# Second attention with three query chunks side by side, and a bit-mask exponential for more key-block pairs on VectorE

## The chip, the cores and the metric

One core of a Trainium2 chip runs the whole program. The metric is the device time of one execution in microseconds, the median of several runs. One further execution was recorded by the hardware profiler; its span, groups, waits and timelines are what this document calls the profile and the trace.

## The reference

Four layers with residuals act on x (2048 tokens, 1024 features, bf16): a linear attention A, a softmax attention B, and both again with the same weights.

```python
x = A_x
x = x + _A_ref(_layernorm(x, axis=-1), A_wqkv, A_w_phi, A_wo)
x = x + _B_ref(_layernorm(x, axis=-1), B_wqkv, B_wo)
x = x + _A_ref(_layernorm(x, axis=-1), A_wqkv, A_w_phi, A_wo)
x = x + _B_ref(_layernorm(x, axis=-1), B_wqkv, B_wo)
```

B is ordinary attention with 32 heads of 32 features: `scores = q k^T * 32**-0.5`, a softmax over 2048 keys, `o = p v`, and a product with wo. A maps q and k by a learned 32x32 matrix per head and two softmaxes over its features, and then needs only sums over keys. B's exponentials, 32 x 2048 x 2048 of them per attention, are the largest body of elementwise work.

## The kernel before, in words

All tokens stay in SBUF as xT, features on partitions, in four chunks of 512 tokens (NC = 4). Heads go in eight groups g of four. A **turn** (qc, g) is one query chunk with one head group, 32 turns in an attention. A turn has two halves pp; a half has 8 key blocks d times 4 strips j. One **unit** (qc, g, pp, d, j) is a score tile of 128 keys by 512 queries from one 32-row strip, 64 units in a turn. Strips 0 and 1 belong to one block of keys, 2 and 3 to another.

`attention` cuts the units into groups of three (WIDE). Each group is three score matmuls on TensorE (L1034), which use different 32-row strips of the array and so run side by side, into one of two sets of three PSUM banks; then one ScalarE exponential over 128x1536 (L1042) into a bf16 tile of class E. Per half, sixteen weighted-sum steps (L1072) add v and ones times these tiles into PSUM bank 6, four matmuls a step, each in its own 32 columns; L1087 copies the bank out. The denominators go through DRAM (L1117 to L1125) and L1128 scales the result into tiles of class oT, which the output projection reads: b_o in the first attention, b_last in the second.

Some units are taken from ScalarE and computed on VectorE by `exp_dve`. EXTRA lists for each attention which (pp, d) of a turn go there, in pairs of units. Each pair has two score matmuls in strip 3 (L972), into bank 7. Then VectorE takes the power of two apart: it rounds the scaled score by adding a large constant (L977), subtracts to get the fraction (L980), clamps the integer part and turns it into exponent bits (L983, L986), evaluates a cubic (three steps at L991) and multiplies (L994).

Projections share bank 7 and TensorE's time with the attention: b_k makes the keys of a group (copied out at L867, spread by four DMAs at L859), b_v the values, b_q the queries of a turn (L875, then two swapping DMAs, L880 and L881). With turns two chunks wide (`turns`, for both attentions: chunks 0 and 1 alternate over the groups, then chunk 2 over all groups, then chunk 3) the queries of chunks 2 and 3 are made early by q_away (L891), stored to DRAM (L893), and fetched by q_back. In the first attention the linear layer that follows is begun beside it (a_keys and layernorm with `alone`), and its weight slabs of 1 MB share SP's queue (L538).

The order of everything is planned when the program is built. `Sched` holds the operations with a planned duration, dependencies, buffers and a due number (`prio`, ten per turn); it plays them through, the lowest due number first among those ready on an engine, within the quotas of buffers by class (QUOTA), and puts fillers on TensorE (L1290) where it would be too little occupied (SPELL, KEEP). The result is one fixed instruction list per engine. Each engine then runs its list in order and waits only by semaphores.

The two lines that set what goes to VectorE and in what order turns run:

```python
EXTRA = (lambda i: [(0, 2), (1, 2)] if 12 <= i < 17 else [],
         lambda i: ([(0, 2), (1, 2)] if i % 3 else [(0, 2), (0, 5), (1, 4)]) if 16 <= i < 30 else [(i % 2, 2)] if 8 <= i < 16 else [])
...
turns = [(qc, g) for g in range(G) for qc in range(2)] + [(qc, g) for qc in range(2, NC) for g in range(G)]
```

Of the kernel before, what the change touches and what calls it, by code (L numbers as in the profile page):

```python
# [10 lines left out]
ACT = mybir.ActivationFunctionType  # L11
# [8 lines left out]
DH = 32  # L20
# [27 lines left out]
class Sched:  # L48
# [96 lines left out]
    def run(self):  # L145
# [25 lines left out]
        while left:  # L171
# [85 lines left out]
NUMS = 2  # L257
LNN = 4
GATE = (1, 1)
KVG = 0.12  # L260
QUOTA = {"pk": 3, "pv": 2, "kv": 1, "ln": 2, "mm": 2, "cmp": 2, "bc": 4, "num": NUMS, "wt": 4, "fil": 2,
         "e": 6, "vp": 6, "e1": 4, "vp1": 4, "E": 6, "q2": 3, "kt": 3, "w2": 8, "w2o": 3, "oT": 26, "T": 4, "den": 2,
         "lnt": 6, "lnw": 2, "lnw1": 1, "eq": 8, "ns": 4, "cw": 6, "hl": 6, "oc": 2, "slab": 7, "slabk": 3, "fin": 4,
         "rs": 8, "pkf": 1, "cden": 2, "part": 8, "w2r": 1,
         "xs": 1, "xu": 2, "xg": 2, "xx": 2, "E1": 3}
SPELL = 3.4
KEEP = 0.75

ROUND = 1.5 * 2**21
POW2_D = 0.32318750170670074  # L270
POW2_0 = 0.998010015430466
POW2_C = (-2.753493604392706, 3.611980637904819, -2.738565741928622)
LEAD = 5.0
EXTRA = (lambda i: [(0, 2), (1, 2)] if 12 <= i < 17 else [],
         lambda i: ([(0, 2), (1, 2)] if i % 3 else [(0, 2), (0, 5), (1, 4)]) if 16 <= i < 30 else [(i % 2, 2)] if 8 <= i < 16 else [])

# [5 lines left out]
def dve_us(n):  # L282
    return n / 960 + 0.15
# [6 lines left out]
def kernel(  # L290
# [19 lines left out]

    q_scale = float(DH**-0.5 / (4 * math.log(2)))

# [646 lines left out]
    def exp_dve(qc, g, pp, d, prio, kT, q_of):  # L959


        u_b, u_v = sb("xu", 2, C512, dt=F32)
        g_b, g_v = sb("xg", 2, C512, dt=F32)
        x_b, x_v = sb("xx", 2, C512, dt=F32)
        e_b, e_v = sb("E1", 2, C512)
        r = slice(96, 128)
        gs = []
        for k in range(2):
            s_b, s_v = ps("xs", FIL)

            def sfn(k=k, s_v=s_v):
                nc.tensor.matmul(  # L972
                    out=s_v(), lhsT=kT[g][1]()[r, pp, (d + k) * P:(d + k + 1) * P],
                    rhs=q_of[(qc, g)][1]()[r, (pp + 1) % 2, :], start=True, stop=True, tile_position=(96, 0))
            so = op("PE", MM, sfn, flat([kT[g][2][(d + k) // 2], q_of[(qc, g)][2]]),
                    [s_b, kT[g][0], q_of[(qc, g)][0]], prio, mode="r")
            uo = op("DVE", dve_us(512), lambda k=k, s_v=s_v: nc.vector.tensor_scalar(  # L977
                out=u_v()[:, k, :], in0=s_v(), scalar1=POW2_D, scalar2=ROUND, op0=ALU.add, op1=ALU.add),
                [so], [s_b, u_b], prio + 0.01)
            gs.append(op("DVE", dve_us(512), lambda k=k, s_v=s_v: nc.vector.scalar_tensor_tensor(  # L980
                out=g_v()[:, k, :], in0=u_v()[:, k, :], scalar=ROUND, in1=s_v(), op0=ALU.subtract, op1=ALU.subtract),
                [uo], [s_b, u_b, g_b], prio + 0.01))
        wo = op("DVE", 1024 / 1920 + 0.15, lambda: nc.vector.tensor_scalar(  # L983
            out=u_v(), in0=u_v(), scalar1=ROUND - 31.5, scalar2=ROUND + 32.0, op0=ALU.max, op1=ALU.min),
            gs, [u_b], prio + 0.02)
        wo = op("DVE", 1024 / 1920 + 0.15, lambda: nc.vector.tensor_scalar(  # L986
            out=u_v().bitcast(I32), in0=u_v(), scalar1=ROUND - 31.75, scalar2=float(2**25),
            op0=ALU.subtract, op1=ALU.mult), [wo], [u_b], prio + 0.02)
        last = gs
        for i, c in enumerate(POW2_C):  # L990
            last = [op("DVE", dve_us(1024), lambda i=i, c=c: nc.vector.scalar_tensor_tensor(  # L991
                out=x_v(), in0=(x_v() if i else g_v()), scalar=c, in1=g_v(), op0=ALU.add, op1=ALU.mult),
                last, [g_b, x_b], prio + 0.02)]
        eo = op("DVE", dve_us(1024), lambda: nc.vector.scalar_tensor_tensor(  # L994
            out=e_v(), in0=x_v(), scalar=POW2_0, in1=u_v(), op0=ALU.add, op1=ALU.mult),
            [wo, *last], [x_b, u_b, e_b], prio + 0.02)
        return eo, (e_b, lambda: e_v().rearrange("p a b -> p (a b)"))

    def attention(base, kT, vT, q_of, gate, extra):
# [7 lines left out]
        for qc, g in turns:  # L1007
            for pp, d in extra(pos[(qc, g)]):
                eo, (e_b, e_v) = exp_dve(qc, g, pp, d, base + 10 * pos[(qc, g)] + 5 * pp + 0.5 * d - LEAD, kT, q_of)
                for k in range(2):  # L1010
                    ex_of[(qc, g, pp, d + k, 3)] = eo
                    e_of[(qc, g, pp, d + k, 3)] = (e_b, e_v, k)
        units = [u for u in units if u not in ex_of]
        n = 0
        i = 0
        while i < len(units):
# [14 lines left out]
            def sfn(grp=grp, s_v=s_v):  # L1031
# [10 lines left out]
            ex = op("ACT", act_us(w * C512), lambda s_v=s_v, e_v=e_v, w=w: nc.scalar.activation(  # L1042
                out=e_v()[:, 0:w * C512], in_=s_v(), func=ACT.Exp, scale=4 * math.log(2)),
                [so], [s_b, e_b], prio - 3)
# [6 lines left out]
        if True:  # L1051
            for qc, g in turns:
                T = []
                end = (qc, g) == turns[-1]
                for pp in range(2):
                    a_b, a_v = ps("acc", [(6,)])
                    last = None
                    for d in range(8):
                        prio = base + 10 * pos[(qc, g)] + 5 * pp + 0.5 * d
                        for u in range(2):  # L1060
# [4 lines left out]
                            def fn(us=us, kc=kc, u=u, d=d, a_v=a_v, v_v=v_v, g=g, pp=pp):  # L1065
                                for k in range(2):
                                    eb, ev, x = e_of[us[k]]
                                    j = 2 * pp + k
                                    for what in range(2):
                                        col = 64 * ((pp + what) % 2) + 32 * k  # L1070
                                        o = (g % 4) * P + j * DH
                                        nc.tensor.matmul(  # L1072
                                            out=a_v()[col:col + 32, :],
                                            lhsT=v_v()[:, kc % 4, o:o + DH] if what == 0 else ones_bf[:],
                                            rhs=ev()[:, x * C512:(x + 1) * C512],
                                            start=(d == 0 and u == 0), stop=(d == 7 and u == 1),
                                            tile_position=(0, col), skip_group_check=True)
# [5 lines left out]
                            last.accum = (d, u) != (7, 1)  # L1083
                    if end and pp:
# [51 lines left out]

    turns = [(qc, g) for g in range(G) for qc in range(2)] + [(qc, g) for qc in range(2, NC) for g in range(G)]
    pos = {t: i for i, t in enumerate(turns)}
    xnA, xnB = {}, {}
# [20 lines left out]
    for layer in range(2):  # L1160
        base = BASE[layer]
        second = base + (100, 45)[layer]
        last = layer == 1
# [36 lines left out]
        for c in range(NC):  # L1200
# [5 lines left out]
            a_out(c, pr + 22, wo_s, oc)  # L1206
            xnB[c] = layernorm(c, pr + 23, ANY, n=LNN if c == NC - 1 else 2)
# [5 lines left out]
        gate = [lnq[-1]] if GATE[layer] else []  # L1213
        at = second + 130

        for g in range(1, G):
            pr = at + 10 * pos[(0, g)] - 19
            w = slab("w2", pr - 1, B_w[:, :, D + g * P:D + (g + 1) * P], P)
            for c in range(NC):
                b_k(g, c, pr + 4 * c, w, kT, FIL, "DVE")  # L1220
        for c in range(NC):
            for t in range(TB):
                b_v(1, c, t, at + 4.5 * (4 * c + t) + 2, bv_s[1], vT, FIL, "DVE")
        for g in range(G):
            pr = at + 10 * pos[(0, g)]
            w = slab("w2", pr - 11, B_w[:, :, g * P:(g + 1) * P], P) if g else wq0
            for qc in range(NC):
                if qc < 2:
                    if qc or g:
                        q_of[(qc, g)] = b_q(g, qc, pr + 10 * qc - 8, w, FIL)  # L1230
                else:
                    away = q_away(g, qc, pr + 2 + 6 * (qc - 2), w, FIL)
                    q_of[(qc, g)] = q_back(g, qc, at + 10 * pos[(qc, g)] - 12, away)
        oTs, last_s = attention(at, kT, vT, q_of, gate, EXTRA[layer])
        if last:
            bo_s = [slab("slab", at + 160 + fc, B_o[:, :, fc * C512:(fc + 1) * C512], C512) for fc in range(2)]
        for qc, p0, gap in ((0, 163, 1.5), (1, 176, 1.5), (2, 251, 1.5)):
            if last:
                gap = (6, 6, 9)[qc]
                p0 = (163, 200, 251)[qc]  # L1240
                for t in range(TB):
# [84 lines left out]
```

## Time and profile before

| what | value |
|---|---|
| median of 3 runs | 2449.53 us (2446.66 to 2449.86) |
| the profiled execution's own time | 2446.52 us |
| its span | 2444.7 us |
| first score exponential of the first, second attention | 354.3 us, 1541.6 us from the span's start |
| ScalarE after the last score exponential of the first attention | next at 1310.7 us |
| score exponentials of three units (L1042) | 1332 |
| fillers on TensorE (L1290) | 2296 matmuls |
| pairs on VectorE | 50 (100 score matmuls at L972) |

How to read the profile: the page gives busy time of each engine over the span and in 40 slices (a digit is tenths of a slice); then groups of instructions by line: count, busy time, mean duration of one in ns, the engine's idle time just before them and what ended it. PE is TensorE's matmuls, PEld its weight loads, DVE VectorE, ACT ScalarE, SP the queue that issues DMAs. A row of the stretches gives its ends and length in us, then busy time with the number of instructions of PE, PEld, DVE, ACT and POOL, the granted clock, and the DMAs' share and GB/s. A row of waits gives who waited for whom, the total in us, how often, and the longest. A timeline row gives start, length, engine, line and operation, and in brackets the idle time before it with what ended it. Matmuls overlap, so their durations (380 ns) are longer than their pitch.

### The profile page before, as it was taken

What the parts mean: (1) busy time and instruction counts of PE and PEld (TensorE: products, weight loads), DVE (VectorE), ACT (ScalarE), POOL (GpSimd) and SP (SyncE); (2) the same over time, 40 slices, a digit from 0 to 9 for tenths busy, and PEclk for the clock granted to TensorE, in tenths of its full rate; (3) what the DMA queues carried; (4) which work ended last, traced back from release to release, by engine and by line L of the source; (5) the groups of instructions that cost most, each with busy time, mean ns of one, the idle gap of its engine ahead of it and who ended that gap; (6) DMA issues with size and microseconds to landing.
All of it is one profiled execution on the core that took longest, in us unless ns stands there. A gap on an engine that the chain in (4) does not pass through costs nothing.

```text
span 2444.7 us, 65791 instructions
## 1 busy us (share of the span) xinstructions
PE 2298.8 (94%) x29160; PEld 848.7 (35%) x29160; DVE 1337.6 (55%) x1775; ACT 2128.3 (87%) x1891; POOL 22.0 (1%) x70
## 2 busy tenths in 40 slices
PE   7999999999989999899999999999999998998998
PEld 4443333333333333333333333333333333333333
DVE  6986752222256635533425766322255478788863
ACT  6336569999999999999996555799999999999998
POOL 0000000000000000000000000000000000000000
PEclk9999999999999999999999999999999999999999
DMA  9210101112111122222324001111121100100000
GB/s 208 62 36 3 31 20 39 39 42 51 37 58 45 45 65 76 75 71 72 123 59 125 1 5 40 32 43 37 40 64 28 37 30 26 35 31 28 27 23 32
DMA packets 204773, 118.59 MB, mean 49 GB/s; under 512 B 122824, under 2 KB 194504, under 8 KB 203720
## 3 DMA queue, kind: packets, MB, share of 16 engines
q1 hardware_dynamic: 203432, 112.29, 17.0%
q8 instruction: 228, 3.74, 0.6%
q10 hardware_dynamic: 1056, 2.10, 0.3%
q14 instruction: 57, 0.47, 0.1%
HBM read 78.71 MB, written 16.24 MB: 39 GB/s over the span
## 4 chain that ended last, share of the span: by engine, by line
ACT 43%; PE 35%; issue 10%; DVE 7%; DMA 3%; SPq 2%; ACTq 0%; DVEq 0%
ACT arena L1042 42%; PE psum L434 19%; PE psum L1072 5%; PE psum L438 4%; PE psum L1034 4%; DVE arena L991 2%; DMA arena<-rd 1%; SPq L469 1%; PE psum L1290 1%; DVE arena L1128 1%; ACT arena L638 1%; PE psum L804 1%; PE psum L671 1%; DVE arena L977 1%; DVE arena L1087 1%
## 5 line engine op out<-in xcount | busy, mean ns | idle before, releaser
L1042 ACT ACTIVATE arena<-psum 128x1536 bf16<-128x1536 f32 x1332 | 1798.7, 1677 | 15.1 <-PE psum L1034 7.6
L1072 PE MATMUL psum<-arena 128*32 128x512 bf16 x4096 | 657.1, 385 | 8.8 <-DVE arena L1087 4.9
L1072 PE MATMUL psum<-arena,ones_bf 128*32 128x512 bf16 x4096 | 656.8, 386 | 2.3 <-issue 2.3
L1034 PE MATMUL psum<-arena 32*128 32x512 bf16 x3996 | 525.1, 383 | 97.1 <-ACT arena L1042 88.9
L438 PE MATMUL psum<-arena 128*32 128x512 bf16 x8256 | 578.6, 381 | 3.8 <-DVE arena L530 0.8
L434 PE MATMUL psum<-arena 128*128 128x512 bf16 x2032 | 472.5, 384 | 10.5 <-DVE arena L1108 3.1
L1034 PEld LDWEIGHTS <-arena 32*128 32x128 bf16 x3996 | 175.5, 91 | 624.6 <-issue 613.1
L434 PEld LDWEIGHTS <-arena 128*128 128x128 bf16 x2032 | 191.0, 98 | 268.7 <-issue 58.2
L438 PEld LDWEIGHTS <-arena 128*32 128x32 bf16 x8256 | 204.1, 96 | 211.4 <-issue 64.8
L1072 PEld LDWEIGHTS <-arena 128*32 128x32 bf16 x4096 | 156.4, 94 | 277.7 <-issue 250.8
L867 DVE CAST arena<-psum 128x512 bf16<-128x512 f32 x112 | 77.2, 689 | 259.2 <-PE psum L438 246.2
L991 DVE SCALAR_TENSOR_TENSOR arena<-arena 128x1024 f32<-128x1024 f32 x150 | 183.4, 1222 | 7.4 <-PE psum L438 2.5
L1290 PE MATMUL psum<-xT,zero 128*32 128x512 bf16 x2296 | 182.9, 380 | 0.0
L1072 PEld LDWEIGHTS <-ones_bf 128*32 128x32 bf16 x4096 | 153.9, 94 | 16.1 <-issue 7.4
L1087 DVE COPY arena<-psum 128x512 f32<-128x512 f32 x126 | 86.6, 687 | 97.3 <-PE psum L1072 96.2
L1128 DVE TENSOR_TENSOR arena<-arena 64x512 bf16<-64x512 f32 x124 | 84.6, 682 | 59.5 <-DMA arena<-rd 46.7
L638 ACT ACTIVATE arena<-psum 128x512 bf16<-128x512 f32 x80 | 42.8, 598 | 79.4 <-PE psum L434 65.7
L651 DVE TENSOR_TENSOR arena<-psum,arena 128x1024 bf16<-128x1024 f32 x64 | 78.3, 1224 | 59.2 <-PE psum L438 53.2
L977 DVE TENSOR_SCALAR arena<-psum 128x512 f32<-128x512 f32 x100 | 68.9, 689 | 69.9 <-PE psum L972 61.8
L642 DVE TENSOR_REDUCE arena<-arena 128x32 f32<-128x1024 bf16 x64 | 77.7, 1214 | 48.6 <-ACT arena L638 48.6
L761 ACT ACTIVATE arena<-psum 128x512 bf16<-128x512 f32 x128 | 69.4, 595 | 34.1 <-PE psum L434 33.6
L526 DVE TENSOR_TENSOR arena<-xT,arena 128x1024 f32<-128x1024 bf16 x64 | 77.9, 1218 | 31.3 <-ACT arena L515 31.2
(102 smaller groups left out, 1295.9 us busy)
## 6 DMA issues: line engine op xcount, KB each, us to landing
arena<-rd SPq DMA_DIRECT2D x62, 256.0 KB
arena<-in_A_wqkv_dram SPq DMA_DIRECT2D x10, 1024.0 KB
arena<-in_B_wqkv_dram SPq DMA_DIRECT2D x32, 256.0 KB
arena<-arena SPq DMA_DIRECT2D x256, 32.0 KB
arena<-in_B_wo_dram SPq DMA_DIRECT2D x32, 256.0 KB
arena<-wd_k SPq DMA_DIRECT2D x8, 1024.0 KB
arena<-in_B_wqkv_dram SPq DMA_DIRECT2D x4, 1024.0 KB
arena<-arena SPq DMA_DIRECT2D x64, 64.0 KB
```

Source lines behind the costliest of these rows:

```text
L434: nc.tensor.matmul(out_, lhsT=lhsT, rhs=rhs, start=start, stop=stop, skip_group_check=True)
L438: nc.tensor.matmul(out_[ks, :], lhsT=lhsT[:, ks], rhs=rhs, start=start, stop=stop, tile_position=(0, 32 * k), skip_group_check=True)
L526: s1 = op("DVE", dve_us(1024), lambda pr=pr, w_v=w_v: nc.vector.tensor_tensor(out=w_v(), in0=xT[:, pr, csl(c)], in1=m_v().unsqueeze(1).to_ ...
L651: ml = op("DVE", dve_us(1024), lambda vpv=vpv, wv_=wv_, sv=sv: nc.vector.tensor_tensor(out=wv_()[:, :, :, 0:DH], in0=vpv().rearrange("p (h ...
L977: uo = op("DVE", dve_us(512), lambda k=k, s_v=s_v: nc.vector.tensor_scalar(out=u_v()[:, k, :], in0=s_v(), scalar1=POW2_D, scalar2=ROUND, o ...
L991: last = [op("DVE", dve_us(1024), lambda i=i, c=c: nc.vector.scalar_tensor_tensor(out=x_v(), in0=(x_v() if i else g_v()), scalar=c, in1=g_ ...
L1034: nc.tensor.matmul(out=s_v()[:, x * C512:(x + 1) * C512], lhsT=kT[g][1]()[r, pp, d * P:(d + 1) * P], rhs=q_of[(qc, g)][1]()[r, (pp + j // ...
L1042: ex = op("ACT", act_us(w * C512), lambda s_v=s_v, e_v=e_v, w=w: nc.scalar.activation(out=e_v()[:, 0:w * C512], in_=s_v(), func=ACT.Exp, s ...
L1072: nc.tensor.matmul(out=a_v()[col:col + 32, :], lhsT=v_v()[:, kc % 4, o:o + DH] if what == 0 else ones_bf[:], rhs=ev()[:, x * C512:(x + 1) ...
L1087: cp = op("DVE", dve_us(512), lambda t_v=t_v, a_v=a_v: nc.vector.tensor_copy(out=t_v(), in_=a_v()), [last], [a_b, t_b], prio - 4)
L1128: s = [op("DVE", dve_us(512), lambda a=a, k=k, o_v=o_v, r_v=r_v, T=T: nc.vector.tensor_tensor(out=o_v()[a, :], in0=T[k][1]()[a, :], in1=r_ ...
L1290: nc.tensor.matmul(psum[32 * k:32 * k + 32, 6 * C512:7 * C512], lhsT=zero[:], rhs=xT[:, 0, 0:C512], start=False, stop=False, tile_position ...
```

## The change

- In the second attention three chunks run side by side (SIDE): turns go over chunks 0, 1 and 2 for each head group, then chunk 3 over all groups. No queries go through DRAM there; those of chunk 3 are made by b_q one turn ahead (LATE), with their weight slabs loaded again. The values of the second half of the heads (VGAP), the output projections (OP0, OGAP) and their slabs (BO) get new due numbers. The first attention keeps two chunks.
- VectorE takes strips 2 and 3 of one key block (d) where it took strip 3 of two blocks (d, d+1). The weighted-sum steps of those pairs go last in their half, so that start and stop follow the order n.
- The exponential itself: the score, scaled by 2**23/ln 2 in q_scale, is added to a constant and clamped at 0 with an int32 output (one step per unit from PSUM); one mask takes the mantissa and sets the exponent of 1, another keeps the exponent; three cubic steps and a product follow.
- EXTRA: 18 pairs in the first attention (turns 10 to 18, two each) and 54 in the second (turns 3 to 29, two each).
- Keys are due five earlier; quotas and one planned duration (KVG) are set anew.

```diff
-KVG = 0.12
+KVG = 0.14
...
-         "xs": 1, "xu": 2, "xg": 2, "xx": 2, "E1": 3}
+         "xs": 1, "xu": 2, "xg": 1, "xx": 1, "E1": 3}
...
+SIDE = (2, 3)
+VGAP = 7.0
+LATE = 10.0
+BO = 225
+OP0 = (233, 259, 285)
+OGAP = (3.2, 3.2, 3.2)
+EXTRA = (lambda i: [(0, 2), (1, 2)] if 10 <= i < 19 else [],
+         lambda i: [(0,2),(1,4)] if 3 <= i < 30 else [])
...
-    q_scale = float(DH**-0.5 / (4 * math.log(2)))
+    q_scale = float(DH**-0.5 / math.log(2) * BITS)
...
-                    out=s_v(), lhsT=kT[g][1]()[r, pp, (d + k) * P:(d + k + 1) * P],
-                    rhs=q_of[(qc, g)][1]()[r, (pp + 1) % 2, :], start=True, stop=True, tile_position=(96, 0))
+                    out=s_v(), lhsT=kT[g][1]()[r, pp, d * P:(d + 1) * P],
+                    rhs=q_of[(qc, g)][1]()[r, (pp + 1) % 2, :], start=True, stop=True,
+                    tile_position=(64 + 32 * k, 0))
...
-            uo = op("DVE", dve_us(512), lambda k=k, s_v=s_v: nc.vector.tensor_scalar(
-                out=u_v()[:, k, :], in0=s_v(), scalar1=POW2_D, scalar2=ROUND, op0=ALU.add, op1=ALU.add),
-                [so], [s_b, u_b], prio + 0.01)
-            gs.append(op("DVE", dve_us(512), lambda k=k, s_v=s_v: nc.vector.scalar_tensor_tensor(
-                out=g_v()[:, k, :], in0=u_v()[:, k, :], scalar=ROUND, in1=s_v(), op0=ALU.subtract, op1=ALU.subtract),
-                [uo], [s_b, u_b, g_b], prio + 0.01))
+            ys.append(op("DVE", dve_us(512), lambda k=k, s_v=s_v: nc.vector.tensor_scalar(
+                out=y_v()[:, k, :].bitcast(I32), in0=s_v(), scalar1=POW2_B, scalar2=0.0, op0=ALU.add, op1=ALU.max),
+                [so], [s_b, y_b], prio + 0.01))
+        mo = op("DVE", 1024 / 1920 + 0.15, lambda: nc.vector.tensor_scalar(
+            out=m_v().bitcast(I32), in0=y_v().bitcast(I32), scalar1=0x7FFFFF, scalar2=0x3F800000,
+            op0=ALU.bitwise_and, op1=ALU.bitwise_or), ys, [y_b, m_b], prio + 0.02)
+        po = op("DVE", 1024 / 1920 + 0.15, lambda: nc.vector.tensor_scalar(
+            out=y_v().bitcast(I32), in0=y_v().bitcast(I32), scalar1=0x7F800000, scalar2=None,
+            op0=ALU.bitwise_and), [mo], [y_b], prio + 0.02)
...
+                    own = extra(pos[(qc, g)])
+                    order = [(d, u) for d in range(8) for u in range(2) if not (u and (pp, d) in own)]
+                    order += [(d, 1) for d in range(8) if (pp, d) in own]
...
+        wide = SIDE[layer]
+        turns = [(qc, g) for g in range(G) for qc in range(wide)] + [(qc, g) for qc in range(wide, NC) for g in range(G)]
...
-            pr = at + 10 * pos[(0, g)] - 19
+            pr = at + 10 * pos[(0, g)] - 24
...
-                b_k(g, c, pr + 4 * c, w, kT, FIL, "DVE")
+                b_k(g, c, pr + 2 * wide * c, w, kT, FIL, "DVE")
...
-                else:
+                elif wide == 2:
...
+        if wide == 3:
+            for g in range(G):
+                pl = at + 10 * pos[(NC - 1, g)] - LATE
+                after = q_of[(NC - 1, g - 2) if g > 1 else (2, G - 1)][2][0]
+                wl = slab("w2", pl - 3, B_w[:, :, g * P:(g + 1) * P], P, [after])
+                q_of[(NC - 1, g)] = b_q(g, NC - 1, pl, wl, FIL)
```

More of the change, by code (lines that the diff above doesn't have):

```diff
@@ L983, in exp_dve @@
[L983 to L989, printed above, removed]
+            ys.append(op("DVE", dve_us(512), lambda k=k, s_v=s_v: nc.vector.tensor_scalar(
+                out=y_v()[:, k, :].bitcast(I32), in0=s_v(), scalar1=POW2_B, scalar2=0.0, op0=ALU.add, op1=ALU.max),
+                [so], [s_b, y_b], prio + 0.01))
@@ new lines, in exp_dve @@
+        mo = op("DVE", 1024 / 1920 + 0.15, lambda: nc.vector.tensor_scalar(
[4 more added lines that the diff above has]
+            op0=ALU.bitwise_and), [mo], [y_b], prio + 0.02)
+        last = [mo]
@@ L990, in exp_dve @@
         for i, c in enumerate(POW2_C):
             last = [op("DVE", dve_us(1024), lambda i=i, c=c: nc.vector.scalar_tensor_tensor(
-                out=x_v(), in0=(x_v() if i else g_v()), scalar=c, in1=g_v(), op0=ALU.add, op1=ALU.mult),
-                last, [g_b, x_b], prio + 0.02)]
+                out=x_v(), in0=(x_v() if i else m_v()), scalar=c, in1=m_v(), op0=ALU.add, op1=ALU.mult),
+                last, [m_b, x_b], prio + 0.02)]
         eo = op("DVE", dve_us(1024), lambda: nc.vector.scalar_tensor_tensor(
-            out=e_v(), in0=x_v(), scalar=POW2_0, in1=u_v(), op0=ALU.add, op1=ALU.mult),
@@ L996, in exp_dve @@
-            [wo, *last], [x_b, u_b, e_b], prio + 0.02)
+            out=e_v(), in0=x_v(), scalar=POW2_0, in1=y_v(), op0=ALU.add, op1=ALU.mult),
+            [po, *last], [x_b, y_b, e_b], prio + 0.02)
         return eo, (e_b, lambda: e_v().rearrange("p a b -> p (a b)"))
@@ L1042, in attention @@
             ex = op("ACT", act_us(w * C512), lambda s_v=s_v, e_v=e_v, w=w: nc.scalar.activation(
-                out=e_v()[:, 0:w * C512], in_=s_v(), func=ACT.Exp, scale=4 * math.log(2)),
+                out=e_v()[:, 0:w * C512], in_=s_v(), func=ACT.Exp, scale=math.log(2) / BITS),
                 [so], [s_b, e_b], prio - 3)
@@ L1057, in attention @@
                     last = None
-                    for d in range(8):
-                        prio = base + 10 * pos[(qc, g)] + 5 * pp + 0.5 * d
-                        for u in range(2):
+                    own = extra(pos[(qc, g)])
+                    order = [(d, u) for d in range(8) for u in range(2) if not (u and (pp, d) in own)]
+                    order += [(d, 1) for d in range(8) if (pp, d) in own]
+                    for n, (d, u) in enumerate(order):
+                        prio = base + 10 * pos[(qc, g)] + 5 * pp + 0.5 * (n // 2)
+                        if True:
                             us = [(qc, g, pp, d, 2 * u + k) for k in range(2)]
@@ L1075, in fn @@
                                             rhs=ev()[:, x * C512:(x + 1) * C512],
-                                            start=(d == 0 and u == 0), stop=(d == 7 and u == 1),
+                                            start=(n == 0), stop=(n == 15),
                                             tile_position=(0, col), skip_group_check=True)
@@ L1082, in attention @@
                                       [a_b, v_b, *ebs], prio - 1, mode="c")
-                            last.accum = (d, u) != (7, 1)
+                            last.accum = n != 15
                     if end and pp:
@@ L1133, in attention @@
         return oTs, so
-    turns = [(qc, g) for g in range(G) for qc in range(2)] + [(qc, g) for qc in range(2, NC) for g in range(G)]
-    pos = {t: i for i, t in enumerate(turns)}
     xnA, xnB = {}, {}
@@ L1161 @@
         base = BASE[layer]
+        wide = SIDE[layer]
+        turns = [(qc, g) for g in range(G) for qc in range(wide)] + [(qc, g) for qc in range(wide, NC) for g in range(G)]
+        pos = {t: i for i, t in enumerate(turns)}
         second = base + (100, 45)[layer]
@@ L1212 @@
                 b_v(0, c, t, pr + 43 + 0.1 * t, bv_s[0], vT, ANY, "ACT")
[L1213 removed]
+        gate = [lnq[-1]]
         at = second + 130
         for g in range(1, G):
[L1217 removed]
+            pr = at + 10 * pos[(0, g)] - 24
             w = slab("w2", pr - 1, B_w[:, :, D + g * P:D + (g + 1) * P], P)
             for c in range(NC):
[L1220 removed]
+                b_k(g, c, pr + 2 * wide * c, w, kT, FIL, "DVE")
         for c in range(NC):
             for t in range(TB):
[L1223 removed]
+                b_v(1, c, t, at + (4.5, VGAP)[wide - 2] * (4 * c + t) + 2, bv_s[1], vT, FIL, "DVE")
         for g in range(G):
@@ L1227 @@
             for qc in range(NC):
-                if qc < 2:
+                if qc < wide:
                     if qc or g:
                         q_of[(qc, g)] = b_q(g, qc, pr + 10 * qc - 8, w, FIL)
-                else:
+                elif wide == 2:
                     away = q_away(g, qc, pr + 2 + 6 * (qc - 2), w, FIL)
                     q_of[(qc, g)] = q_back(g, qc, at + 10 * pos[(qc, g)] - 12, away)
+        if wide == 3:
[4 more added lines that the diff above has]
+                q_of[(NC - 1, g)] = b_q(g, NC - 1, pl, wl, FIL)
         oTs, last_s = attention(at, kT, vT, q_of, gate, EXTRA[layer])
         if last:
-            bo_s = [slab("slab", at + 160 + fc, B_o[:, :, fc * C512:(fc + 1) * C512], C512) for fc in range(2)]
+            bo_s = [slab("slab", at + BO + fc, B_o[:, :, fc * C512:(fc + 1) * C512], C512, [q_of[(2, G - 1)][2][0]])
+                    for fc in range(2)]
         for qc, p0, gap in ((0, 163, 1.5), (1, 176, 1.5), (2, 251, 1.5)):
             if last:
-                gap = (6, 6, 9)[qc]
-                p0 = (163, 200, 251)[qc]
+                gap = OGAP[qc]
+                p0 = OP0[qc]
                 for t in range(TB):
```

32 lines of the change are left out of this document (14 added, 18 removed).

## The prediction

> **What bounds the kernel now.** I read the busy totals and the slices first, then the costliest groups, then each attention by itself. From the page:
>
> ```profile
> PE 2298.8 (94%) x29160; PEld 848.7 (35%) x29160; DVE 1337.6 (55%) x1775; ACT 2128.3 (87%) x1891; POOL 22.0 (1%) x70
> ...
> ACT  6336569999999999999996555799999999999998
> ...
> L1042 ACT ACTIVATE arena<-psum 128x1536 bf16<-128x1536 f32 x1332 | 1798.7, 1677 | 15.1 <-PE psum L1034 7.6
> ...
> L1290 PE MATMUL psum<-xT,zero 128*32 128x512 bf16 x2296 | 182.9, 380 | 0.0
> ```
>
> TensorE's 94% is not the bound: 2296 of its matmuls (L1290) are fillers that the planner adds only to keep it awake; four run side by side, so 2296/4 x 0.217 = 124 us are no work. ScalarE's slices show two plateaus of 9, the two attentions, made of 1332 exponentials, each over three units of 128x512 scores. Stretches by engine and the waits, first attention (374 to 1295 us), then second (1565 to 2433):
>
> ```profile
> 374.00:1295.00 921.00, 864.22 (x12720) 305.48 (x12721) 373.79 (x500) 910.49 (x712) 8.31 (x24) 1.00 0.22 61
> 1565.00:2433.00 868.00, 813.55 (x11341) 282.46 (x11333) 515.73 (x666) 866.14 (x645) 0.00 (x0) 1.00 0.12 34
> ```
> ```profile
> ACT arena L1042 <- PE psum L1072: 5.9, 6, 1.5
> ACT arena L1042 <- PE psum L1034: 4.4, 6, 1.2
> ```
> ```profile
> L1042 ACT ACTIVATE arena<-psum 128x1536 bf16<-128x1536 f32 x645 | 867.2, 1692 | 1.5 <-PE psum L1072 1.5
> ```
>
> ScalarE is the fourth number: busy 910.5 of 921 and 866.1 of 868 us. It waited 10.3 us in the first attention (the pair of wait lines) and 1.5 in the second. So an attention lasts as long as ScalarE has exponentials, one group every 866.14/645 = 1.343 us, 0.448 us a unit. The mean of 1677 ns is longer because neighbours overlap. Outside the attentions TensorE binds, and the change leaves that work as it is.
>
> **The change, part by part.**
>
> *44 units leave ScalarE.* VectorE now takes 50 pairs (10 and 40), then 72 (18 and 54): 44 units more, 16 in the first attention and 28 in the second. By the instruction lists ScalarE goes from 1332 groups of three to 1316 and two of two: 44 x 0.448 = **19.7 us** less, on the path as long as ScalarE stays fed (7.2 + 12.5).
>
> *VectorE's chain.* The rows that price it:
>
> ```profile
> L991 DVE SCALAR_TENSOR_TENSOR arena<-arena 128x1024 f32<-128x1024 f32 x150 | 183.4, 1222 | 7.4 <-PE psum L438 2.5 <-PE psum L1072 1.3 <-PE psum L1034 0.3
> ...
> L977 DVE TENSOR_SCALAR arena<-psum 128x512 f32<-128x512 f32 x100 | 68.9, 689 | 69.9 <-PE psum L972 61.8 <-ACT arena L1042 5.8 <-PE psum L1072 1.1
> L980 DVE SCALAR_TENSOR_TENSOR arena<-arena,psum 128x512 f32<-128x512 f32 x100 | 68.7, 687 | 4.2 <-PE psum L1072 0.2
> L994 DVE SCALAR_TENSOR_TENSOR arena<-arena 128x1024 bf16<-128x1024 f32 x50 | 61.1, 1222 | 2.7
> ...
> L983 DVE TENSOR_SCALAR arena<-arena 128x1024 f32<-128x1024 f32 x50 | 34.7, 693 | 1.6
> L986 DVE TENSOR_SCALAR arena<-arena 128x1024 int32<-128x1024 f32 x50 | 34.6, 693 | 1.5
> ```
>
> A pair costs 2 x 0.689 + 2 x 0.687 + 2 x 0.693 + 4 x 1.222 = 9.03 us now. The new one drops the two L980 steps; its two mask steps (integers in and out) have no row. They cost 0.69 us each by L983/L986, where 1024 elements with one tensor input take half of L991's time, and 1.22 by L991. I take 0.69: L986 already writes int32 at that speed. So 7.65 us, 8.7 at the other end. Second attention: 54 x 7.65 - 40 x 9.03 = 52 us more VectorE work on 515.7 us, thus about 568 of 855, and spread over 27 turns of 60 units (26.9 us) instead of crowded behind turn 16. VectorE is not the bound, and ScalarE's time hides the chain while its result is ready before the weighted sum asks. There the lists help: in the second attention between a pair's second score matmul and its use stand at least 6 score groups in both kernels (8.1 us); the rest of the chain was 0.689 + 0.687 + 1.39 + 4.89 = 7.65 us and becomes 6.96. Cost 0. With 1.22 us masks it is 8.0, and the nine or so pairs with 6 or 7 groups come up to 1 us late: 0 to 9 us.
>
> *Even pairs.* VectorE took head 3 of two neighbouring key blocks; now it takes heads 2 and 3 of one. ScalarE's groups are cut from what is left, and where a seam falls badly a group holds two units of one head, which use the same 32 rows of TensorE and cannot run side by side. Counting them through the loops: none before, 18 + 27 = 45 now. Each holds its scores up by one more matmul. What room there is, from the ScalarE timeline and the score triples (second attention):
>
> ```profile
> 1650.75 3.19 ACT L1042 ACTIVATE arena<-psum 128x1536 bf16<-128x1536 f32 x2
> ```
> ```profile
> 1652.12 3.16 ACT L1042 ACTIVATE arena<-psum 128x1536 bf16<-128x1536 f32 x2
> ```
> ```profile
> 1650.09 0.39 PE L1034 MATMUL psum<-arena 32*128 32x512 bf16 x3
> 1651.30 0.40 PE L1034 MATMUL psum<-arena 32*128 32x512 bf16 x3
> ```
>
> Scores ending at 1650.48 and 1651.70 serve exponentials that start at 1650.75 and 1652.12: 0.27 and 0.42 us to spare. The chain of waits prices the extra matmul by matmuls that all use the same full set of rows:
>
> ```profile
> 1489.92 22.12 PE psum L434 x102
> ```
>
> 22.12/102 = 0.217 us, weights loaded meanwhile. That mostly fits the room: I take 1 us in all, between 0 and 45 x 0.217 = 9.8.
>
> A worse mechanism would be that the second unit's weights can't be loaded while the first streams: a load and a whole matmul each, 91 + 383 ns by L1034's groups on the page = 0.47 us, 21 us in all. The chain line, same rows all along at 0.217 us, does not bear it out for full-width weights; whether strips behave alike no run shows yet.
>
> That mechanism is a rule of the Trainium skill, "TensorE: Matmul & The Clock Gate", section "Part 3: Packing small matmuls — row/col tiling": a weight load overlaps running matmuls only where its row group differs. By that rule the sum below would be 2449, no difference.
>
> *Three chunks side by side.* A head group's three turns now span about 81 us instead of 57, so projections of the next group spread; the 16 trips of queries through DRAM (64 DMAs) in the second attention go, 32 swaps and 8 weight slabs come, 24 fewer issues on SP. Queries for turns 16 to 31 used to be ready over 170 groups early; now every turn's are made shortly before. By the lists the fewest groups between a query's last matmul and its turn are 4, 5, 6, 6 (turns 11, 12, 8, 9). Four are 5.4 us; the chain is 0.69 (L875) + a second issue 0.59 + a small transfer (copy done at 396.63, its reader starts at 399.10: 2.5 us), 3.8 us. Cost 0 while VectorE takes it at once. In the first attention a new order of fillers leaves 1 group instead of 4 ahead of turn 1: about 3.8 - 1.3 - 0.4 = 2 us (0 to 4). Output projections of chunks 0 to 2 all move behind turn 24: counted from the list, TensorE's work without fillers rises there to 19 to 24 us per 20 groups (26.9 us of ScalarE). The first 40 groups of this attention carry 26 and 24.5 now and lose only 1.4 us of ScalarE. Cost 0, up to 8. Behind the last scores 20 fewer weighted-sum and 16 fewer projection matmuls stand (list): 0.5 us gained, 0 to 2.
>
> *First attention's stalls.* Its 10.3 us come where big weight slabs share the queue:
>
> ```profile
> 702.93 0.69 DVE L867 CAST arena<-psum 128x512 bf16<-128x512 f32 x1 [6.96 <-DMA qd<-arena]
> ```
>
> A query store issued at 696.0, 3 us behind two slab loads, took 7 us, and a buffer and then ScalarE waited. The slabs stay and are only reshuffled: 0, plus or minus 4.
>
> **Sum**, against the profiled execution's 2446.5 us (span 2444.7 + 1.8): -19.7 + 1 + 2 - 0.5 = 2429.3. That execution is 3.0 below the median shown (2449.5); I go half-way: **2431**. Its own range by these ends is 2425 to 2438.
>
> **Rivals.**
> - *Masks at L991's speed.* For: no row has integer inputs. Against: L986. Late pairs, up to 9 us: 2438.
> - *The repeated strips cost all of it.* For: 25% of scores may have under 0.27 us to spare, as the first pair above. Against: the second pair. 9.8 us instead of 1: 2440 (0.04); with the weights waiting too, 21 us: 2451, no difference (0.01).
> - *TensorE has no room left in the last turns.* 24 of 26.9 us plus late seams; if the last 150 groups lose 0.1 us each, 15 us go: 2445, no difference. Against: the 1.4 us above.
> - *Slower: query copies stand behind VectorE's chain.* In the second attention VectorE works in order; a query's copy that finds a whole chain ahead of it is late by 7.65 us, and its swaps by the 7 us transfer above at worst: 0.7 + 7.65 + 0.6 + 7 = 16 us against 1.343 us for each group of lead. Summed over the fifteen turns with leads of 12 or less, that is up to 58 us. From a third of that (20 us) the gain is gone; at half to two thirds: 2465. For: the second attention loses its early queries, and VectorE's mean load rises. Against: seven turns with leads of 4 to 10 already run there with no more than 0.6 us stalls, and large slabs come there only near turn 23.
>
> **Chances.** Forecast 0.62; masks 0.09; strips 0.04 and 0.01; no room 0.08; late queries 0.16. About 0.2% (4.9 us) is what a measurement here can tell from no change, so faster means under 2444.6: 0.62 + 0.09 + 0.04 = 0.75; same 0.08 + 0.01 = 0.09; slower 0.16. The range takes in forecast, masks, strips and most of no room: 2424 to 2447.
>
> **What would show it.** ScalarE busy near 99% in both attentions, 1318 exponentials, 1.343 us per group; the mask rows at 690 and not 1220 ns; VectorE under 85% everywhere in the second attention; ScalarE's waits for score matmuls below 15 us in all. Wrong would be idle on ScalarE at starts of turns 8 to 12 (late queries), after seams (strips), or from turn 24 on (no room).

## The result, and the profile after

The changed kernel takes 2427.12 us (median of 4 runs, 2425.31 to 2429.2) against 2449.7 for the old one beside it: a ratio of 0.9911, 95% interval 0.9894 to 0.9928, 22.6 us less. The profiled execution took 2425.63 us, its span is 2423.8; against the old one's profiled 2446.52 that is 20.9 us less, where the sum of the prediction had 17.2.

From the page of the changed kernel (lines moved by the diff: L1042 is now L1044, L1034 L1036, L1072 L1077, L1290 L1303):

```profile
PE 2288.1 (94%) x28846; PEld 843.1 (35%) x28916; DVE 1432.4 (59%) x1851; ACT 2110.5 (87%) x1877; POOL 22.1 (1%) x70
...
ACT  6336559999999999999997455799999999999998
...
L1044 ACT ACTIVATE arena<-psum 128x1536 bf16<-128x1536 f32 x1318 | 1780.5, 1613 | 14.1 <-PE psum L1036 6.6
...
L1303 PE MATMUL psum<-xT,zero 128*32 128x512 bf16 x2120 | 170.2, 381 | 0.8 <-DVE xT L931 0.8
```

ScalarE has 14 exponentials less and waits 14.1 us before them, as it did before (15.1). VectorE's 1432 us are 95 more. The two attentions by stretch, then ScalarE's group in the second one:

```profile
374.00:1290.00 916.00, 866.92 (x12694) 305.21 (x12686) 421.63 (x549) 908.20 (x710) 8.39 (x24) 1.00 0.23 62
```
```profile
1555.00:2412.00 857.00, 811.39 (x11169) 277.86 (x11166) 564.74 (x698) 853.66 (x635) 0.00 (x0) 1.00 0.12 32
```
```profile
L1044 ACT ACTIVATE arena<-psum 128x1536 bf16<-128x1536 f32 x635 | 854.3, 1612 | 3.1 <-PE psum L1077 1.6 <-PE psum L1036 1.4
```

ScalarE is still busy 99.1% and 99.6% of them, one group in 853.66/635 = 1.344 us. VectorE's 564.7 us are the forecast 568. Where the 20.9 us came from, by the starts and ends of ScalarE's exponentials in both traces:

| stretch | before, us | after, us | difference | forecast |
|---|---|---|---|---|
| up to the first exponential | 354.3 | 354.8 | +0.5 | 0 |
| first attention | 955.7 | 946.6 | -9.1 | -5.2 |
| between the attentions | 231.6 | 229.4 | -2.2 | 0 |
| second attention | 891.0 | 881.1 | -9.9 | -11.5 |
| behind the last exponential | 12.1 | 12.0 | -0.1 | -0.5 |

The stretch between has the same work in both. TensorE sets it, and the granted clock differs (the last but two numbers of these rows, old kernel, then changed):

```profile
1309.80:1541.40 231.60, 225.22 (x1577) 90.32 (x1576) 155.04 (x213) 120.80 (x202) 2.59 (x8) 0.98 0.08 19
```
```profile
1301.10:1530.50 229.40, 219.87 (x1549) 89.78 (x1574) 155.21 (x213) 120.77 (x202) 2.59 (x8) 0.99 0.07 20
```

The trace of the old kernel has 10.2 us at half clock there (granted clock 0.5), that of the changed one 3.4: half of the difference, 3.4 us of TensorE's time, covers the 2.2. What decides how much of it an execution has stays open. The twelve experiments below leave the work of this stretch as it is, and theirs takes 228.4 us (none at half clock) to 231.2 us, so 2.2 us need no cause in the change: the forecast had nothing for them, and they are luck.

### The profile page after: what moved, and what is told of

Same layout as the page of the kernel before. It is cut to its first block, busy times and chain, and to the rows that moved or that the text cites. A ratio compares the mean times of both kernels' runs of the same rounds, so it can differ in the third digit from the quotient of the medians.

```text
span 2423.8 us, 65196 instructions
## 1 busy us (share of the span) xinstructions
PE 2288.1 (94%) x28846; PEld 843.1 (35%) x28916; DVE 1432.4 (59%) x1851; ACT 2110.5 (87%) x1877; POOL 22.1 (1%) x70
## 3 DMA queue, kind: packets, MB, share of 16 engines
q1 hardware_dynamic: 207144, 110.19, 17.2%
## 4 chain that ended last, share of the span: by engine, by line
ACT 36%; PE 20%; issue 8%; DVE 8%; DMA 2%; SPq 0%; ACTq 0%; DVEq 0%; another core or an unknown queue 0%
ACT arena L1044 35%; PE psum L438 8%; PE psum L1077 4%; PE psum L1036 3%; PE psum L442 3%; DVE arena L993 3%; DVE arena L1133 1%; PE psum L1303 1%; ACT arena L642 1%; DMA arena<-arena 1%; DMA arena<-rd 1%; DVE arena L1092 1%; DVE arena L982 1%; DVE arena L985 1%; PE psum L976 1%
## 5 line engine op out<-in xcount | busy, mean ns | idle before, releaser
L1044 ACT ACTIVATE arena<-psum 128x1536 bf16<-128x1536 f32 x1318 | 1780.5, 1613 | 14.1 <-PE psum L1036 6.6
L1077 PE MATMUL psum<-arena 128*32 128x512 bf16 x4096 | 657.0, 385 | 12.3 <-DVE arena L1092 9.3
L1077 PE MATMUL psum<-arena,ones_bf 128*32 128x512 bf16 x4096 | 657.0, 385 | 0.0
L1036 PE MATMUL psum<-arena 32*128 32x512 bf16 x3952 | 529.4, 383 | 76.1 <-ACT arena L1044 67.1
L438 PE MATMUL psum<-arena 128*128 128x512 bf16 x1970 | 464.2, 383 | 15.7 <-DVE arena L1113 3.6
L1036 PEld LDWEIGHTS <-arena 32*128 32x128 bf16 x3952 | 170.6, 91 | 580.0 <-issue 568.2
L993 DVE SCALAR_TENSOR_TENSOR arena<-arena 128x1024 f32<-128x1024 f32 x216 | 264.0, 1222 | 8.6 <-PE psum L442 2.1
L1077 PEld LDWEIGHTS <-arena 128*32 128x32 bf16 x4096 | 160.6, 94 | 291.0 <-issue 257.2
L1303 PE MATMUL psum<-xT,zero 128*32 128x512 bf16 x2120 | 170.2, 381 | 0.8 <-DVE xT L931 0.8
L1077 PEld LDWEIGHTS <-ones_bf 128*32 128x32 bf16 x4096 | 156.5, 94 | 20.3 <-issue 14.2
L982 DVE TENSOR_SCALAR arena<-psum 128x512 int32<-128x512 f32 x144 | 99.4, 690 | 92.0 <-PE psum L976 80.5
```

Of the source, the lines that this page charges most:

```text
L438: nc.tensor.matmul(out_, lhsT=lhsT, rhs=rhs, start=start, stop=stop, skip_group_check=True)
L982: ys.append(op("DVE", dve_us(512), lambda k=k, s_v=s_v: nc.vector.tensor_scalar(out=y_v()[:, k, :].bitcast(I32), in0=s_v(), scalar1=POW2_B ...
L1036: nc.tensor.matmul(out=s_v()[:, x * C512:(x + 1) * C512], lhsT=kT[g][1]()[r, pp, d * P:(d + 1) * P], rhs=q_of[(qc, g)][1]()[r, (pp + j // ...
L1077: nc.tensor.matmul(out=a_v()[col:col + 32, :], lhsT=v_v()[:, kc % 4, o:o + DH] if what == 0 else ones_bf[:], rhs=ev()[:, x * C512:(x + 1) ...
L1303: nc.tensor.matmul(psum[32 * k:32 * k + 32, 6 * C512:7 * C512], lhsT=zero[:], rhs=xT[:, 0, 0:C512], start=False, stop=False, tile_position ...
```

## The experiments

All are edits of the changed kernel, and the planner makes a new list for each. Times are medians; differences are to 2427.1. The old kernel, run beside the three batches of experiments, took 2446.6, 2447.9 and 2448.6 us where it took 2449.7 beside the changed one, so a difference of some 3 us says nothing; the ratios in brackets are to the old kernel of the same batch.

**No pairs.** `EXTRA = (lambda i: [], lambda i: [])`

> The changed kernel with no pair on VectorE in either attention, all 4096 units on ScalarE; turns, due numbers and everything else as changed. Theory (the time follows the number of units on ScalarE, 0.448 us each): 144 units come back, 64.5 us above the changed kernel's 2427.1, so 2492 (2488 to 2497). Rival (the gain came from the new order of turns and the loss of the trips through DRAM): the 21 to 23 us stay gained against the old kernel with its 100 units put back, 2449.7 + 44.8 - 22 = 2472 or so.

2492.7 (ratio to the old kernel 1.0185, 1.0167 to 1.0202). 65.6 us for 144 units, 0.456 each: the theory, and far from the rival. That it agrees so closely is in part luck: ScalarE waits 5.5 us there behind the two 1 MB slabs of the output projection, where the changed kernel waits 0.5. Without these 5.0 us a unit is worth 0.42.

**Fifty pairs.**

```diff
+EXTRA = (lambda i: [(0, 2), (1, 2)] if 12 <= i < 17 else [],
+         lambda i: [(0,2),(1,4)] if 3 <= i < 23 else [])
```

> The changed kernel with the old number of pairs: 10 in the first attention (turns 12 to 16) and 40 in the second (turns 3 to 22, two each), all else as changed. Theory (count of units): 44 units back on ScalarE, 19.7 us more than 2427.1: 2447 (2443 to 2451), within the noise of the old kernel. Rival (order of turns, shorter chain): stays near the changed kernel, 2427 to 2433.

2457.0 (1.0026 to 1.0055): 10 us above what the count gives, a miss of the theory's range. Timeline of ScalarE and waits of TensorE there:

```profile
2144.65 1.45 ACT L1044 ACTIVATE arena<-psum 128x1536 bf16<-128x1536 f32 x1 [6.74 <-PE psum L1036]
```
```profile
PE psum L442 <- DMA arena<-in_B_wqkv_dram: 7.0, 1, 7.0
```

A query's weight slab was issued right behind the two 1 MB slabs of the output projection; TensorE stood at the projection for 7 us, and with it the next scores. That stall and its neighbours are the excess. The same slabs return below.

**Two chunks side by side in both attentions.** `SIDE = (2, 2)`

> The changed kernel with two chunks side by side in both attentions, as the old one had; the new chain, the even pairs and all 72 pairs stay. Theory (only the count matters, the order of turns pays nothing by itself): 2428 (2424 to 2434). Rival (three chunks make the room in which VectorE can take two pairs in every turn from 3 on; with two chunks its projections crowd the first 16 turns): ScalarE waits for late results, over 2437.

2471.8 (1.0080 to 1.0114), 44.7 more: the rival. The loss is all in the second attention (922.7 us against 881.1), from turn 5 to 14, where projections are densest. This prices two chunks with the pairs, and the output projections' due numbers, where the change put them; no run has two chunks with the pairs behind turn 16, where most of the old kernel's were.

**The old chain.** The old exp_dve and its constants with strips 2 and 3 of one block.

> The changed kernel with the old exponential on VectorE (rounding constant, 9.03 us a pair by the rows, 8.3 us of it behind the pair's second score in the new pairing) for all 72 pairs; even pairs and turns as changed. Theory (the chain is hidden): pairs with six groups of lead (8.1 us) come up to 0.5 us late, so 2427 to 2435. Rival (the shorter chain is what let VectorE take 44 units more): VectorE's 72 x 1.38 = 99 us more show on ScalarE wherever VectorE is over 90% busy, 2440 to 2470.

2474.9 (1.0101 to 1.0134), 47.8 more: by its size the rival, 5 us beyond its range. But VectorE is nowhere over 90% busy, as the rival had it: in stretches of 72 to 83 us of the second attention it is at 82% at most. With two buffers each for xg and xx, as the old kernel had, the planner makes the same list, so those quotas are not the cause.

**Masks twice, scores read twice.** The two ways in which the old chain is dearer, taken apart:

```diff
+        mo = op("DVE", 1024 / 1920 + 0.15, lambda: nc.vector.tensor_scalar(
+            out=m_v().bitcast(I32), in0=y_v().bitcast(I32), scalar1=0x7FFFFF, scalar2=0x3F800000,
+            op0=ALU.bitwise_and, op1=ALU.bitwise_or), [mo], [y_b, m_b], prio + 0.02)
...
```

> The changed kernel with each of the two mask steps issued twice (same values), 2 x 0.69 = 1.39 us more per pair on VectorE, all of it from SBUF: a pair costs 9.04 us like the old chain, but holds PSUM bank 7 no longer than the new one. Theory A (what the old chain costs is bank 7, which each of its units holds for two reads, 1.90 us instead of 1.11 in the traces, and which the projections need): little, 2427 to 2440. Theory B (VectorE's time and the chain's length, 8.3 us behind the second score against 6 groups = 8.1 us): like the old chain's 2475, over 2455.

```diff
+            ys.append(op("DVE", dve_us(512), lambda k=k, s_v=s_v: nc.vector.tensor_scalar(
+                out=y_v()[:, k, :].bitcast(I32), in0=s_v(), scalar1=POW2_B, scalar2=0.0, op0=ALU.add, op1=ALU.max),
+                [ys[-1]], [s_b, y_b], prio + 0.01))
```

> The changed kernel with the step that reads the scores from PSUM issued twice per unit (same values): 2 x 0.69 = 1.38 us more per pair on VectorE as in the run with masks twice, but behind the second score only 0.69 us of it, and bank 7 is held about 0.8 us longer per unit. Theory A (bank 7): near the old chain's 2475, over 2455. Theory B (VectorE's time): as much as the run with masks twice; if it is the chain's length, less than that run, 2427 to 2450.

2468.6 (1.0064 to 1.0094) and 2481.7 (1.0118 to 1.0148). So 1.39 us more of VectorE's time per pair costs 41.5 us although bank 7 is held no longer (1.12 us a unit): theory B, and of it VectorE's time. The 13 us more of the run with scores read twice, where a unit holds the bank for 1.84 us, can't be put on the bank. In the second attention that run is 6.3 us longer than masks twice, and 3.8 of these ScalarE loses behind the 1 MB slabs of the output projection:

```profile
2202.53 1.45 ACT L1047 ACTIVATE arena<-psum 128x1536 bf16<-128x1536 f32 x1 [4.61 <-PE psum L1039]
```

Of the first attention's 7.1 us, 5.3 stand at 982 to 988 us, behind its last pair, at a stretch of 6.8 us at half clock. The old chain holds the bank as long (1.90 us), and the planner gives it the same list for the second attention; it is 3.2 us longer there than masks twice, with 3.6 more lost at the same slabs. What holding the bank costs by itself stays open and may be nothing; nor does the chain's length behind the second score order the runs. A stretch of turns 8 to 12 of the second attention, masks twice, then the changed kernel:

```profile
1765.00:1920.00 155.00, 143.29 (x1899) 47.73 (x1897) 122.21 (x153) 139.51 (x104) 0.00 (x0) 0.98 0.12 29
```
```profile
1755.00:1890.00 135.00, 127.48 (x1692) 42.65 (x1689) 103.85 (x126) 134.61 (x101) 0.00 (x0) 1.00 0.11 29
```

In the first row ScalarE is idle for 15 of 155 us, yet VectorE is busy only 79% (77% in the changed kernel), and TensorE's 143 us hold 26 us of fillers (L1309): no engine is full. What is full, by the lists, are tiles. The instruction lists tell how many score groups TensorE issues ahead of a weighted-sum step beyond the newest one that the step uses. Usually it is 2. Six or more, as many as there are result tiles of class E, come at 8 steps of the second attention in the changed kernel, 45 with masks twice, 50 with the old chain, 37 with two chunks; and they come at turns 8 to 12 and 25 to 31 with masks twice, 5 to 14 with two chunks, where ScalarE idles. The largest wait of ScalarE with masks twice, from 1700 us on, is for weighted sums (L1083):

```profile
ACT arena L1050 <- PE psum L1083: 21.5, 15, 3.6
```

This is read as follows: a late pair holds the weighted sums, tiles stay taken, ScalarE stops. No run gives masks twice more tiles, which would test it directly; the next ones change the tiles of the changed kernel.

**Tiles.** `"E": 6` to `"E": 5`, then `"E": 8` with `"E1": 4`:

> The changed kernel with five result tiles (class E) for ScalarE's groups instead of six. Theory (a late VectorE result holds the weighted sums, and ScalarE can then go on only as far as it has tiles, so the room for lateness is about six groups; with five it is one group = 1.34 us less): 5 to 20 us more, 2432 to 2447. Rival (the weighted sums follow two groups behind nearly everywhere, tiles are never short): 2427 plus or minus 3.

2448.5 (0.9991 to 1.0009 of the old kernel), 21.4 more, a little beyond the theory's range: one tile less takes the whole gain. Two places make up most of it, both at large slabs. Waits at the second, VectorE's, TensorE's, ScalarE's:

```profile
DVE arena L1127 <- DMA arena<-arena: 7.7, 2, 7.1
```
```profile
PE psum L976 <- DVE arena L982: 6.3, 1, 6.3
```
```profile
ACT arena L1044 <- PE psum L1077: 8.4, 2, 6.9
```

The small transfers of a turn's denominators were issued 5 us behind the slabs, with two weight slabs of 256 KB between; VectorE, in order, stood at their reciprocal for 7.1 us, a pair's scores behind it, the weighted sum behind that, and ScalarE ran out of tiles.

> The changed kernel with eight result tiles for ScalarE and four for VectorE's pairs instead of six and three. Theory (more room for late results): 2 to 7 us less, 2420 to 2425; only a few places in the changed kernel's list reach the six. Rival (no place in which tiles are short still matters): 2427 plus or minus 2.

2432.7 (0.9923 to 0.9948), 5.6 more, at the edge of what can be told (the changed kernel's interval ends at 0.9928): the theory's gain did not come. The second attention is 2.3 us shorter (878.8), but the first 3.3 longer (949.9), by stalls behind its slabs.

**Repeated strips.** First none, then nearly all:

```diff
+        for i in range(0, len(units) - 8, 3):
+            if len({u[4] for u in units[i:i + 3]}) < 3:
+                k = next(k for k in range(i + 3, i + 8) if units[k][4] not in (units[i][4], units[i + 1][4]))
+                units[i + 2], units[k] = units[k], units[i + 2]
```

> The changed kernel with the units reordered so that none of ScalarE's groups holds two units of one head (the 45 groups swap their third unit with a later one). Theory (a repeat costs one more matmul, 0.195 us in the changed kernel's trace, mostly within ScalarE's room): 1 to 2 us less than 2427, not told apart from it (2422 to 2430); score groups all near 0.39 us. Rival (each repeat also waits for its weights and delays ScalarE by most of 0.47 us): 10 to 20 us less, 2407 to 2417.

2433.2 (0.9921 to 0.9954), 6 more instead of 1 to 2 less, again at the edge of what can be told, and outside both ranges. At the 45 groups ScalarE loses 0.3 us instead of 2.1, so the repeats did cost 1.8. But the new list has the read of a turn's denominators behind the two 1 MB slabs, and VectorE's timeline shows what that does:

```profile
2134.44 1.41 DVE L1137 TENSOR_TENSOR arena<-arena 64x512 bf16<-64x512 f32 x2 [5.71 <-DMA arena<-rd]
```

In the changed kernel that read is issued 0.6 us ahead of the slabs. ScalarE loses 5.1 us more here, and the first attention is 3.4 longer.

```diff
+        units.sort(key=lambda u: (pos[(u[0], u[1])], u[2], u[3] // 2, u[4], u[3]))
```

> The changed kernel with the units of two neighbouring key blocks taken head by head, so that 1273 of the 1318 groups hold two units of one head instead of 45. Theory (0.195 us more per group, of which ScalarE feels the part beyond its room: about 0.05 us a group in the second attention, nothing in the first): 20 to 70 us more, 2445 to 2495. Rival (0.47 us each, beyond nearly every group's room of 0.3 to 0.55): 150 us more or beyond, over 2570.

2743.1 (1.1187 to 1.1221), by its size the rival. But its repeats are no longer than the changed kernel's (0.59 us for the three matmuls); about a quarter of ScalarE's groups start late, by 0.85 us on average (276.1 us in 323 waits for scores), and the others by nearly nothing. This order also keeps a result tile until both key blocks are summed, so it takes tiles away as well, and does not price repeats; what its 316 us are made of is not shown. Hence one that moves no unit further than a group:

```diff
+        for i in range(0, len(units) - 5, 6):
+            k = next((k for k in range(i + 3, i + 6) if units[k][4] in (units[i][4], units[i + 1][4])), None)
+            if k is not None and len({u[4] for u in units[i:i + 3]}) == 3:
+                units[i + 2], units[k] = units[k], units[i + 2]
```

> The changed kernel with the third unit of every other group swapped with one of the next group so that 658 groups hold two units of one head (45 before), while no unit moves further than one group; the run with all repeats mixed eight units and so also held ScalarE's result tiles longer. Theory (0.195 us more per repeat, mostly inside ScalarE's room; 0 to 0.055 us felt each, as in the changed kernel's two attentions): 613 x that, 2427 to 2461. Rival (what the run with all repeats lost, 0.25 us per repeat, is the price of a repeat): 150 us more, 2575 or beyond.

2480.1 (1.0119 to 1.0147), 53 us for 613 repeats more, 0.086 us each at most (stalls at slabs are in it too): above the theory's range, far below the rival. Two neighbouring score triples of this run, the second a repeat:

```profile
1707.40 0.39 PE L1040 MATMUL psum<-arena 32*128 32x512 bf16 x3
1708.70 0.60 PE L1040 MATMUL psum<-arena 32*128 32x512 bf16 x3
```

A repeat takes 0.2 us more.

**Eight tiles, and the old due number for the first attention's keys.**

```diff
+            pr = at + 10 * pos[(0, g)] - (19 if wide == 2 else 24)
```

> As the run with eight and four tiles, and in the first attention the keys have their old due number (19 instead of 24 ahead), which puts the query of turn 1 four groups ahead of its turn again instead of one. Theory: the gap of 2.2 us at the start of turn 1 of the first attention goes, 1 to 3 us below the run with eight tiles. Rival (the gap comes back elsewhere in the new order): the same as that run.

2424.6 (0.9895 to 0.9924): 8 us below the run with eight tiles alone, more than the theory's 1 to 3, and not told apart from the changed kernel. The gap at turn 1 is gone. The profiled executions differ by 5.1 us, 4.9 of them in the first attention: the gap, and stalls that fell otherwise.

## Why the prediction was right, point by point

- **44 units off ScalarE, 19.7 us: right.** No pairs at all gives 0.456 us a unit against 0.448 (0.42 without the wait at the slabs), and with fifty pairs, so without the 44 units, nothing of the gain is left.
- **Chain 7.65 us, cost 0: right in size, wrong about its margin.** The mask steps, integer in and out, go at the speed of L983 and L986, so that rival falls:

```profile
L988 DVE TENSOR_SCALAR arena<-arena 128x1024 int32<-128x1024 int32 x72 | 49.9, 693 | 2.3
L985 DVE TENSOR_SCALAR arena<-arena 128x1024 int32<-128x1024 int32 x72 | 49.8, 692 | 4.3 <-PE psum L1077 0.5
```

  But its price, "0 to 9 us" for 1.06 us more per pair, was far too small: 1.39 us more cost 41.5. The step that failed took VectorE's mean load (568 of 855 us) for room and counted only pairs with the least lead. VectorE's load itself was forecast well: its busiest stretch of 73 us is 80% full, under the 85% named. By the lists, ScalarE's waits and the run with five tiles, the room is the six result tiles, and the planner's list already contains ScalarE's waits when they run out. (A slip that changes nothing: the 2438 of this rival is counted from 2429.3, the 2440 of the strips from 2431.)
- **Bank 7 was left out.** From a unit's score matmul to the end of VectorE's last read the trace has 1.90 us with the old chain and 1.11 with the new (medians, second attention). The prediction counts VectorE's time alone. Whether it had to count more is not shown: what scores read twice cost beyond masks twice is, for the larger part, waits at slabs and at a stretch of half clock.
- **Even pairs, 1 us: 1.8.** A repeated group takes 587 instead of 392 ns, one matmul more, as the chain line of the old kernel said. The rule of the Trainium skill that the prediction weighed ("TensorE: Matmul & The Clock Gate", "Part 3: Packing small matmuls — row/col tiling": weight loads overlap matmuls only in other row groups) would have made it 0.47 us; these strips do not show that, the load (91 ns) is hidden.
- **Three chunks, cost 0: right, but not neutral.** Undone alone it costs 44.7 us. The rival of late queries did not come: turns 8 to 12 lose 0.1 to 0.4 us a turn but for one with 1.1, in spite of leads of 4 to 6 groups. Nor did the one without room on TensorE: from turn 24 on ScalarE's starts slip 4.2 us, 2.7 in the old kernel.
- **First query, 2 us: right.** ScalarE's timeline at turn 1 of the first attention:

```profile
392.61 4.13 ACT L1044 ACTIVATE arena<-psum 128x1536 bf16<-128x1536 f32 x3 [1.97 <-PE psum L1036]
```

- **Slab stalls, 0 plus or minus 4: that size, here in its favour.** The first attention gained 9.1 us where count and query give 5.2. With fifty pairs, as many there as the old kernel had, it takes 953.8 us: 1.9 of the gain come without the count, and 7.2 with the 16 units, as forecast. For the second attention the sum had no term for slabs, and that none was needed is luck: from the issue of the two 1 MB slabs on, ScalarE waits 0.5 us in 30 in the changed kernel, but 5.5 to 8.4 in seven of the twelve experiments, whose lists differ by small edits.
- **The second attention fell 1.6 us short:** ScalarE's starts slip 20.7 us in sum beyond its fastest pitch, 17.9 before.

So the price of a unit carried the forecast; that the total came within 4 us also took luck at the slabs and between the attentions. That all parts had to come together for it (undoing turns, chain or one tile costs more than the 44 units bring) it did not see.

## What to carry to other kernels

Where one engine is full, work taken from it pays its own price per unit, but only as long as the helper's results arrive in time: count the buffers that lie between them, not the helper's mean load. A run that lengthens the helper's step shows this better than its load does. In a fixed order of instructions, look at what stands in a queue right behind a large transfer: transfers of 2 and 256 KB there kept their readers waiting 5 to 7 us in these runs, and an engine that works in order passes that on.

## What the runs showed that was not expected

- VectorE at 79% and ScalarE at 90% busy in one stretch, and TensorE's 92% in part fillers: nothing was full, and the six tiles of 3 KB per partition most likely set the pace. In the changed kernel one less cost 21 us, two more gained nothing.
- A transfer of 2 KB behind two slabs of 1 MB and two of 256 KB kept its reader waiting 7.1 us, a slab of 256 KB right behind the two 7.0.
- A rearrangement that takes a cost away (1.8 us of repeats) can lose three times that by where a transfer falls in the new list; below some 6 us such edits do not tell what they are about.
